# The attention's inputs loaded three items deep instead of four

## The chip, the cores and the metric

The kernel runs on one core of a Trainium2 chip. That core has a matrix engine (PE, with its weight loads shown apart as PEld), a vector engine (DVE), a scalar engine (ACT), a general engine (POOL) and a synchronising engine (SP) which here does nothing but issue DMAs. The five run their own instruction lists and meet only at semaphores. Data move between the large off-chip memory and the on-chip SBUF by sixteen DMA engines, which all queues share. The metric is the time on the device of one execution, in microseconds; lower is better.

## The reference

Two blocks follow one another. The first is a linear attention with decay over 4 batches, 8 heads, 768 steps and head size 48:

```
state = 0                                            # (B, H, D, D)
for t in range(S):
    cur = einsum('bhd,bhe->bhde', u * k[t], v[t])
    y[t] = einsum('bhd,bhde->bhe', r[t], state + cur)
    state = w * state + einsum('bhd,bhe->bhde', k[t], v[t])
```

Its output, with the heads side by side, is `x` (4 x 768 rows of 384). The second block is a mixture of eight experts: each row gets gate logits, an expert is chosen per row (a fresh arg-max, or the expert of the row before, as a local gate says), and the row's result is `p[e] * (relu(x @ w1[e]) @ w2[e])`, with `w1[e]` of 384 x 1024 and `w2[e]` of 1024 x 384. All is float32.

## The kernel before

**Items.** The attention is cut into 16 items, numbered 0 to 15: one item is one batch and one pair of heads (`B * HP`, 4 x 4). An item's 768 steps are six chunks of 128. Each item has three inputs in SBUF: `rk` (r and k, turned, 768 KB), `kv` (k and v by token, 584 KB) and `vT` (v turned, 384 KB). `load(n)` (L191) issues these three DMAs from SP, in that order; item 0's `rk` goes in two halves (L199).

**What an item goes through.** POOL makes three products in `scale(n)` (L205): `rw` (r times the decay, L236), `ke` (k times a decay, from `kv`, L215) and `pd` (r times k, L219). For items 0 to 2, DVE makes `rw` itself. DVE makes `kw` in `keys(n)` (k times the inverse decay, L246); for items 14 and 15 POOL does that too. PE then does `added(n)` (L258, from `ke` and `v`), `scores(n)` (L297, from `rw` and `kw`), `own(n)` (L276, from `pd`), `inside(n)` (L306, with `v` of `kv`) and `before(n)` (L319, from `rw`). DVE multiplies PE's result of `own` by `vT` (L282), masks the scores (L299) and scans the states (L264). ACT copies the result out (L327), PE turns it (L338) and, at the end of each batch, ACT writes `x` to memory with a DMA of its own (L343).

**Order.** The program's order is written out by hand (`manual_schedule`), in `run` (L362): iteration n loads an item ahead, then issues `turn(n-2)`, `added(n)`, `scale(n+1)`, `inside(n-1)`, `before(n-1)`, `scores(n+1)`, `own(n)` and `keys(n+2)`, with exceptions in the first five iterations and with the routing's work in the second half. Engines run ahead of one another as far as buffers let them: `ke`, `pd` and `kw` have two buffers each, `rw` four. Since `pd` of item m+2 goes where `pd` of item m was, POOL's `pd(m+2)` comes after PE's `own(m)`.

**Buffers of the inputs.** `AHEAD` sets how many there are, which one an item takes, and how far ahead `load` runs:

```
104         self.rks, self.vTs = [None] * AHEAD, [None] * AHEAD
105         for i in range(1, AHEAD + 1):
106             self.rks[(n + i) % AHEAD] = once.tile([P, 2, NCH, P], F32, name=f"rk{i}")
109         self.kvs = [once.tile([P, 2 * VB + DP - DH], F32, name=f"kv{i}") for i in range(AHEAD + 1)]
112         for i in range(AHEAD - 1):
113             self.load(i)
114         nc.sync.dma_start(out=self.wp, in_=wp_d)
...
194         rk, vT, kv = self.rks[n % AHEAD], self.vTs[n % AHEAD], self.kvs[n % (AHEAD + 1)]
...
375             if n + AHEAD - 1 < M:
376                 self.load(n + AHEAD - 1)
```

So with four, `rk(n)` and `vT(n)` take the place of item n-4, and `kv(n)` that of item n-5. SP works its list in order: the DMA of `rk(n)` waits until POOL and DVE have done with `rk(n-4)`, `kv(n)` until PE's `inside(n-5)` is through, `vT(n)` until DVE's multiplication after `own(n-4)` is. The weights `wp` (128 KB) are loaded behind the third item (L114).

**After the attention.** The pool that holds these buffers is closed (L522) and the experts' pools are laid where it was. The first thing there is the second set of expert weights, `w1t` and `w2t` (24 KB of each partition), which lies over the four `rk` buffers and is fetched from ACT (L1593, L1104, L1106) while the first expert's rows are computed. The experts are ten blocks of gathered rows, bound by PE, to the end of the kernel.

Of the kernel before, what the change touches and what calls it, by code (L numbers as in the profile page):

```python
# [48 lines left out]

W_LO, W_HI = 0.8, 1.25  # L50
C2 = NCH // 2
AHEAD = 4
VB = NCH * 2 * DH
LATE = (B * HP - 2, B * HP - 1)

# [7 lines left out]
class Attention:  # L63
# [13 lines left out]
    def __init__(self, tc, st, rk_d, kv_d, vT_d, x_d, w_t, wp_d, kept, ident, lt, mp):  # L77
# [25 lines left out]
        n = B * HP - 1  # L103
        self.rks, self.vTs = [None] * AHEAD, [None] * AHEAD
        for i in range(1, AHEAD + 1):
            self.rks[(n + i) % AHEAD] = once.tile([P, 2, NCH, P], F32, name=f"rk{i}")
        for i in range(1, AHEAD + 1):
            self.vTs[(n + i) % AHEAD] = once.tile([P, 2, C2, P], F32, name=f"vT{i}")
        self.kvs = [once.tile([P, 2 * VB + DP - DH], F32, name=f"kv{i}") for i in range(AHEAD + 1)]
        self.items = [dict() for _ in range(B * HP)]  # L110
# [1695 lines left out]
```

## Time and profile before

| | us |
|---|---|
| median of three runs | 377.43 (377.28 to 378.89) |
| the profiled execution | 378.4 |
| its span, first to last instruction | 376.7 |
| PE busy | 361.5 |
| DVE busy | 244.8 |
| POOL busy | 152.3 |
| ACT busy | 110.5 |

The profile's page gives the busy time of each engine and, in 40 slices of 9.42 us, each engine's busy share in tenths, the clock granted to PE, and what the DMA engines moved. The trace behind it answers for any line, tile or stretch: who waited for whom, and each instruction's start and length. In a timeline row the columns are start, length, engine, source line, operation, what is written and read, shape and count; idle time before it and its releaser stand in brackets. The attention takes the first 107 us or so, the experts the rest.

### The profile page before, as it was taken

To read this page: it belongs to the slowest core of one execution; us is meant where nothing else is said; L and a number is where in the kernel's file an instruction comes from. 1 tells how busy PE (TensorE), PEld (TensorE's weight loads), DVE (VectorE), ACT (ScalarE), POOL (GpSimd) and SP (SyncE) were. 2 spreads that over 40 slices of the span, in tenths; PEclk is the share of its full clock that TensorE was granted. 3 is DMA by queue.
4 is the path that set the end of the run, shared out by engine and by line. 5 is a ranking of instruction groups with operands and counts; after the bars stand their busy time and mean duration, and the time that the engine had idled before them with its cause. 6 is when DMAs were issued, how large, how long until landed. Compare 5 with 4: busy or idle time off the path is not lost. (4 is left out here: it accounts for less than half of the span.)

```text
span 376.7 us, 9667 instructions
## 1 busy us (share of the span) xinstructions
PE 361.5 (96%) x3844; PEld 318.7 (85%) x3844; DVE 244.8 (65%) x711; ACT 110.5 (29%) x304; POOL 152.3 (40%) x212
## 2 busy tenths in 40 slices
PE   7998899999999999999999999999999999999992
PEld 6766777777769998989899999999999998989971
DVE  6887778788834835886557666857767767555300
ACT  4222232223523212322332233333243233331210
POOL 8789999789512055212333113313233023021012
PEclk9999999999999999999999999999999999999998
DMA  7999998992568748713352452264165065072011
GB/s 256 411 407 408 404 409 314 338 357 106 196 194 298 269 169 336 260 35 127 121 198 62 155 216 78 56 218 186 36 209 220 14 220 202 19 259 114 2 41 37
DMA packets 17764, 74.93 MB, mean 199 GB/s; under 512 B 2778, under 2 KB 6624, under 8 KB 15408
## 3 DMA queue, kind: packets, MB, share of 16 engines
q1 hardware_dynamic: 10336, 56.89, 40.7%
q0 software_dynamic: 3424, 9.48, 7.3%
q10 hardware_dynamic: 3952, 7.87, 5.6%
q8 instruction: 32, 0.52, 0.6%
q14 instruction: 20, 0.16, 0.1%
HBM read 64.79 MB, written 9.47 MB: 197 GB/s over the span
## 5 line engine op out<-in xcount | busy, mean ns | idle before, releaser
L1358 POOL DMA_INDIRECT out_dram<-yo,sid x27 | 26.6, 985 | 115.8 <-ACT yo L1353 92.3
L1209 PE MATMUL h<-exT,w1t 128*128 128x168 f32 (+4 forms) x240 | 54.9, 327 | 0.0
L1213 DVE TENSOR_TENSOR hT<-h,hs 128x168 f32<-128x168 f32 (+3 forms) x60 | 21.1, 351 | 46.2 <-PE h L1209 29.6
L1132 POOL DMA_INDIRECT xg<-x_d,gid x29 | 31.2, 1076 | 30.3 <-DVE gid L899 19.2
L1209 PEld LDWEIGHTS h<-exT,w1t 128*128 128x128 f32 x240 | 41.6, 190 | 0.3 <-issue 0.3
L1159 PE MATMUL h<-exT,w1t 128*128 128x168 f32 (+2 forms) x192 | 37.3, 332 | 0.0
L299 DVE TENSOR_TENSOR am<-pair,kept 128x768 f32<-128x768 f32 x32 | 30.1, 953 | 11.0 <-PE pair L297 10.8
L1278 PE MATMUL y<-factors,sums 128*128 128x192 f32 x168 | 36.8, 326 | 0.0
L219 POOL TENSOR_TENSOR pd<-rk 128x384 f32<-128x384 f32 x32 | 31.8, 1014 | 8.9 <-PE y L276 6.3
L1209 PE MATMUL h<-xs,ws 128*128 128x168 f32 (+4 forms) x144 | 35.3, 327 | 0.0
L1159 PEld LDWEIGHTS h<-exT,w1t 128*128 128x128 f32 x192 | 30.9, 190 | 2.0 <-issue 0.2
L1278 PEld LDWEIGHTS y<-factors,sums 128*128 128x128 f32 x168 | 29.0, 190 | 0.2
L1209 PEld LDWEIGHTS h<-xs,ws 128*128 128x128 f32 x144 | 25.5, 190 | 4.3 <-ACT hs L1216 1.2
L297 PE MATMUL pair<-rw,kw 48*64 48x128 f32 (+1 forms) x768 | 23.4, 249 | 1.9 <-issue 1.7
L236 POOL TENSOR_TENSOR rw<-rk,tab 128x384 f32<-128x384 f32 x26 | 23.6, 930 | 0.4 <-DMA rk<-in_rk_dram 0.4
L306 PE MATMUL y<-am,kv 128*64 128x128 f32 x360 | 22.9, 276 | 0.3
L1278 PE MATMUL y<-w2t,hT 128*128 128x192 f32 x96 | 23.0, 328 | 0.0
L297 PEld LDWEIGHTS pair<-rw,kw 48*64 48x64 f32 x768 | 19.9, 133 | 3.4 <-issue 2.4
L1146 DVE COPY exT<-tp 128x384 f32<-128x384 f32 (+5 forms) x29 | 13.8, 485 | 13.2 <-PE tp L1145 13.1
L215 POOL TENSOR_TENSOR ke<-kv,endT 128x288 f32<-128x288 f32 (+1 forms) x32 | 21.8, 704 | 0.9 <-DMA kv<-in_kv_dram 0.9
L306 PEld LDWEIGHTS y<-am,kv 128*64 128x64 f32 x360 | 19.4, 137 | 2.2 <-issue 1.1
L327 ACT COPY xT<-y 128x768 f32<-128x768 f32 x15 | 12.0, 801 | 29.0 <-PE y L319 29.0
(304 smaller groups left out, 735.4 us busy)
## 6 DMA issues: line engine op xcount, KB each, us to landing
w1t<-in_w_dram SPq DMA_DIRECT2D x8, 1536.0 KB, 6.9
w2t<-in_w_dram SPq DMA_DIRECT2D x8, 1536.0 KB, 7.4
rk<-in_rk_dram SPq DMA_DIRECT2D x15, 768.0 KB, 10.3
kv<-in_kv_dram SPq DMA_DIRECT2D x16, 584.0 KB, 8.5
vT<-in_vT_dram SPq DMA_DIRECT2D x16, 384.0 KB, 6.3
x_d<-x ACTq DMA_DIRECT2D x4, 1152.0 KB
w1t<-in_w_dram SPq DMA_DIRECT2D x2, 768.0 KB
w2t<-in_w_dram SPq DMA_DIRECT2D x2, 768.0 KB, 5.2
```

What stands on the lines that cost most here:

```text
L215: nc.gpsimd.tensor_mul(t["ke"][:, z], t["k"][:, z], spread(self.endT[:, p, hp], 1, len(range(NCH)[z])))
L219: nc.gpsimd.tensor_mul(t["pd"][:, z], t["rT"][:, z], t["kT"][:, z])
L236: engine.tensor_mul(t["rw"][:, z], t["rT"][:, z], spread(pw, 1, z.stop - z.start))
L297: nc.tensor.matmul(sc[f * DP:(f + 1) * DP, h, i, x:], lhsT=t["kw"][q, c, o * DP:(o + 1) * DP], rhs=t["rw"][q, c, x:], start=True, stop=True)
L299: return lambda: nc.vector.tensor_mul(t["am"][:, g], sc, spread(self.kept[:, g:g + 3], 1, 2))
L306: nc.tensor.matmul(t["y"][h][p * DP:(p + 1) * DP, c2 * P:(c2 + 1) * P], lhsT=t["v"][:, (2 * c + h) * DH:(2 * c + h) * DH + DP], rhs=t["am" ...
L1132: self.nc.gpsimd.indirect_dma_start(out=xg[:n], out_offset=None, in_=self.x_d[:rows], in_offset=bass.IndirectOffsetOnAxis(ap=u["gid"][:n, ...
L1159: nc.tensor.matmul(h[:, :n], lhsT=u["w1"][:, m, kk, :], rhs=u["xT"][:, kk, :], start=(kk == 0), stop=(kk == DK - 1))
L1209: nc.tensor.matmul(out, lhsT=a, rhs=b, start=start and k == 0, stop=stop and k == len(terms) - 1, skip_group_check=True)
L1213: nc.vector.tensor_tensor(out, a, b, op=Alu.add)
L1278: return lambda: nc.tensor.matmul(bank[:, x * half:(x + 1) * half], lhsT=a, rhs=b, start=(j == 0 and x == 0), stop=(j == FK // 2 - 1), ski ...
L1358: self.nc.gpsimd.indirect_dma_start(out=out.rearrange("n (h d) -> (n h) d", h=2) if half else out, out_offset=bass.IndirectOffsetOnAxis(ap ...
```

## The change

One constant is changed:

```
-AHEAD = 4
+AHEAD = 3
```

By the lines above this does five things. There are three `rk` and three `vT` buffers in place of four, and four `kv` in place of five. `rk(n)` and `vT(n)` now follow item n-3, and `kv(n)` item n-4. Before the loop two items are loaded in place of three, so that `wp` stands on SP's list ahead of item 2, not behind it. In iteration n, `load(n+2)` is issued in place of `load(n+3)`. And each partition has 13.6 KB less in that pool (6144 + 3072 + 4672 bytes), so that what follows in it lies lower, and the second set of expert weights lies over three `rk` buffers and two of `vT`. The number of DMAs, their sizes and their order, `wp` apart, stay; so do all instructions of the other engines.

## The prediction

> **What bounds the kernel now.** I read the page first, then a table of stretches, then the waits, then the timeline of SP, POOL and PE. The page:
>
> ```profile
> span 376.7 us, 9667 instructions
> PE   7998899999999999999999999999999999999992
> GB/s 256 411 407 408 404 409 314 338 357 106 196 194 298 269 169 336 260 35 127 121 198 62 155 216 78 56 218 186 36 209 220 14 220 202 19 259 114 2 41 37
> ```
>
> PE is busy to nine tenths nearly throughout. The change touches only the loads of the attention, slices 0 to 10. There the loads move some 408 GB/s until slice 5 ends (56 us). Two stretches of it, with all engines:
>
> ```profile
> core 0: us, PE busy (x) PEld busy (x) DVE busy (x) ACT busy (x) POOL busy (x), PEclk, DMA share, GB/s
> 36.20:62.50 26.30, 24.43 (x587) 19.41 (x587) 19.22 (x42) 7.35 (x20) 24.09 (x30) 1.00 1.01 395
> 62.50:88.00 25.50, 25.01 (x551) 19.34 (x547) 21.43 (x36) 7.04 (x16) 21.22 (x26) 1.00 0.80 293
> ```
>
> PE works 93% and 98% of them, POOL 92% and 83%; the DMA engines are full in the first and 80% busy in the second. PE sets the pace of 5 to 7 us per item, and POOL is not far from it. So the question is whether later inputs make PE wait. The waits of SP's queue and of POOL tell who waits for inputs today:
>
> ```profile
> SPq L201 <- DVE y L282: 24.7, 9, 3.6
> SPq L200 <- PE y L306: 9.7, 6, 4.6
> SPq L201 <- DMA rk<-in_rk_dram: 5.4, 4, 1.5
> POOL pd L219 <- PE y L276: 6.3, 5, 2.4
> POOL pd L219 <- DMA rk<-in_rk_dram: 2.4, 2, 1.4
> POOL ke L215 <- DMA kv<-in_kv_dram: 0.9, 1, 0.9
> POOL rw L236 <- DMA rk<-in_rk_dram: 0.4, 1, 0.4
> ```
>
> SP waits for buffers (the first two rows), early on also for earlier DMAs to land (the third). No PE or DVE row of size names an input. Only POOL waits for inputs: 3.7 us in four waits, all before 27 us. Later POOL waits for PE, because `pd` has two buffers: POOL is ahead of PE and gives its lead up there.
>
> **The change, part by part.** No instruction is added or removed; all cost is in when the loads start.
>
> *Early items (3 to 8).* These are SP's issues of `rk` that matter, and a last reader of item 2's buffer:
>
> ```profile
> 18.36 0.38 SPq L196 DMA_DIRECT2D rk<-in_rk_dram  x1
> 19.67 0.55 DVE L236 TENSOR_TENSOR rw<-rk,mp 128x384 f32<-128x384 f32 x1
> 26.40 0.33 SPq L196 DMA_DIRECT2D rk<-in_rk_dram  x1
> 31.71 0.33 SPq L196 DMA_DIRECT2D rk<-in_rk_dram  x1
> 36.62 0.38 SPq L196 DMA_DIRECT2D rk<-in_rk_dram  x1
> ```
>
> These are items 5, 7, 8 and 9. After the change item 5 waits for item 2's reader, until 20.22: 1.9 us later. Item 7 waits for item 4's, which is the row at 31.71: 5.3 us later. Do these delays reach the data? Landing times, for the issues at 26.4, 31.7 and 58.0 in that order:
>
> ```profile
> DMA to landing us min/median/max: 11.7/11.7/11.7
> DMA to landing us min/median/max: 10.7/10.7/10.7
> DMA to landing us min/median/max: 5.7/5.7/5.7
> ```
>
> The last queue is nearly empty, so 5.7 us is an `rk` behind its predecessor's `vT` alone; the others stood some 6.0 and 5.0 us behind earlier loads. An issue that comes later by less than that finds the same place in the same stream and lands at the same time: 1.9 and 5.3 are below 6.0. Item 8 goes from 31.71 to the slot at 36.62, 4.9 us later, against 5.0. So up to about 42 us data land as before. `wp`, now ahead of item 2, costs that item 128 KB at 408 GB/s, an estimated 0.3 us; POOL's wait of 0.4 us for item 3 takes it up. Sum so far: 0 (at most 0.3).
>
> *From item 9 on, one slot later.* SP's slots are set by the readers (24.7 and 9.7 us above): `vT` and the next `rk` leave when a multiplication at L282 ends. Unless the compute moves, the slots stay and each carries one item less: the slot that took `rk(10)` takes `rk(9)`. Nothing stands ahead then. The slots, and when POOL, the first reader, wants the data:
>
> ```profile
> 46.85 0.39 SPq L196 DMA_DIRECT2D rk<-in_rk_dram  x1
> 52.69 1.69 POOL L236 TENSOR_TENSOR rw<-rk,tab 128x384 f32<-128x384 f32 x2
> 58.01 0.38 SPq L196 DMA_DIRECT2D rk<-in_rk_dram  x1
> 64.14 1.69 POOL L236 TENSOR_TENSOR rw<-rk,tab 128x384 f32<-128x384 f32 x2
> 72.03 0.68 SPq L200 DMA_DIRECT2D kv<-in_kv_dram  x1
> 78.33 1.36 POOL L215 TENSOR_TENSOR ke<-kv,endT 128x288 f32<-128x288 f32 x2
> ```
>
> With 5.7 us: item 9 is there at 52.55 (wanted 52.69), item 11 at 63.7 (64.14). Just in time, both. The slot in the last pair, which takes `kv(13)` in place of `kv(14)`, is the worst, since ACT's write of `x` goes beside the loads from 65 us on. It landed in
>
> ```profile
> DMA to landing us min/median/max: 9.1/9.1/9.1
> ```
>
> So `kv(13)` is there at 81.1, 2.8 us late: **POOL will wait**, some 3 us around 78 us. What does that cost PE?
>
> *The cover.* POOL's lead over PE, and a stretch with the columns of the table above:
>
> ```profile
> 81.55 1.98 POOL L219 TENSOR_TENSOR pd<-rk 128x384 f32<-128x384 f32 x2 [1.85 <-PE y L276]
> 86.58 0.66 PE L258 MATMUL mp<-kv,ke 128*48 128x48 f32 x20
> 93.54 1.96 POOL L246 TENSOR_TENSOR kw<-rk,held 128x384 f32<-128x384 f32 x2
> 97.73 1.27 PE L297 MATMUL pair<-rw,kw 48*64 48x128 f32 x46
> ```
>
> ```profile
> 81.55:95.50 13.95, 13.95 (x296) 10.44 (x296) 11.70 (x23) 5.61 (x16) 13.95 (x16) 1.00 0.42 149
> ```
>
> PE reads `ke(13)`, which POOL has at 79.7 (78.33 + 1.36), at 86.6: a lead of 6.9 us, so 2.8 us late doesn't reach PE there. What runs on in POOL's list is the lateness itself: at 81.55 POOL waits 1.85 us for PE anyway, which takes 2.8 down to about 1.0. From there POOL is without a pause (13.95 of 13.95 us) up to `kw(15)`, ready at 95.5, read by PE at 97.7: a lead of 2.2 us, against 1.0 late. Sum: 0.
>
> DVE reads `rk` after POOL does, in `keys(n)` at the end of iteration n-2; `vT(n)` has three items' time. Neither wants data sooner than POOL.
>
> *Behind the attention.* The second set of expert weights now lies over three `rk` and two `vT`. The last multiplication with any `vT`, and ACT's fetch into that memory:
>
> ```profile
> 102.86 1.17 DVE L282 TENSOR_TENSOR pair<-pair,vT 128x384 f32<-128x384 f32 x2 [0.25 <-PE pair L276]
> 114.68 0.36 ACTq L1104 DMA_DIRECT2D w1t<-in_w_dram  x1
> ```
>
> The readers are done 10 us before; cost 0.
>
> *The sum* is 0 on the profiled execution, 376.7 us of span in 378.4 (1.7 us outside the span, untouched). That execution is 1.0 us over the median of three, so the forecast is the median: 377.4.
>
> Bounds of what no row shows: the landing times with shorter queues. Below, an `rk` takes 5.7 us at best; POOL would then wait less, still for nothing on PE. Above, the longest landing of a `kv` in the trace:
>
> ```profile
> DMA to landing us min/median/max: 5.7/8.5/12.2
> ```
>
> I take 5.7 without and 9.1 us with the write beside it, since those are the very slots.
>
> **Rivals.** *POOL's lead runs out (slower).* Place: `kw(15)`, or `scores(15)` at 97.7. It decides once POOL is over 1.85 + 2.2 = 4.1 us late at 78 us, which is a landing of 10.4 us for the slot at 72.03 (78.33 + 4.1 - 72.03). With the 12.2 of the full queue POOL is 5.9 us late and PE waits 1.8: 379.2. If the next slots are as slow and POOL loses about 1 us more, 380.2. For it: the slot already takes 9.1, and the lateness comes back in SP's slots, as `rk` waits for POOL. Against it: fewer loads are in the queue. The Trainium skill, "Perfetto Trace Analysis", Optimization Strategy, speaks for this rival: the same gap repeating on an engine that should be saturated can mean that buffers for the next tile lack. By that, one buffer less should open one gap per item; the rows put that gap on POOL and not on PE, and no run here yet shows it.
>
> *PE's instruction supply gains (faster).* PE has pauses in which it waits for nothing that the profile shows, here in 24 to 36 and in 36 to 62.5 us, and a queue of instructions shares the DMA engines:
>
> ```profile
> PE pair L297 <- issue: 1.2, 2, 1.0
> PE mp L258 <- issue: 1.7, 2, 1.3
> q8 instruction: 32, 0.52, 0.6%
> ```
>
> The same waits sum to 0.5 us in 62.5 to 88, where the DMA engines are less full. If the pauses are late instructions, an earlier end of the saturation (42 instead of 58 us) saves up to 1.7 us: 375.7; if all 2.9 go, 374.5. Against it: most of the pauses lie before the queue gets shorter. The Trainium skill, "DMA: Bandwidth & Descriptors", Queues, rings and completion order, speaks against it as well: each DMA engine takes its queues in turn, packet by packet, so a long queue should delay another one no more than a short one. No run here shows that.
>
> *The depth isn't in force (no change).* SP's waits for earlier DMAs (5.4 us in the row above) would pace it instead. That holds up to 26 us only; then the same 377.4 would come with unchanged landing times.
>
> **How the numbers follow.** About 0.5%, 1.9 us, is what a measurement of this kernel can tell from no change: 375.5 to 379.3. The forecast (loads one slot later, hidden by POOL's lead) has 0.75; the depth not in force 0.03, at the same time; POOL's lead running out 0.14, about 379.2 to 380.2, of which 0.01 within the bound; the gain of instructions 0.08, about half of it beyond the bound, as only the full 2.9 is past it. That makes faster 0.05, same 0.82, slower 0.13. The range leaves out the far ends of both, 0.05 and some 0.07: 375.7 to 379.7.
>
> **What would show it.** Right: landing times of `rk` near 6 us from item 8 on, where they were 10 to 12 until item 8; DMA share in 36 to 62 us below 1.0; new waits of POOL for `rk` or `kv`, some 3 to 4 us in sum after 50 us, the longest near 78; POOL's waits for PE at L219 shorter by about that much; PE's waits and the start of the experts, at 109 us, as before. Wrong: a wait of PE's L297 or L258 on POOL, and a later start of the experts; or the experts starting earlier with PE's pauses gone. A difference that arises after 109 us would be none of these, and would point to where the tiles lie.

## The result, and the profile after

| | before | after |
|---|---|---|
| median of 21 executions each, on the same chip | 377.52 us (376.46 to 381.29) | 380.49 us (376.30 to 385.54) |
| executions over 379 us | 3 of 21 | 15 of 21 |
| ratio after / before, 95% interval | | 1.0052 [1.0032, 1.0073] |
| the profiled execution | 378.4 us | 377.7 us |

The change makes the kernel about half a per cent slower (0.8% by the medians of all executions), and the forecast, 377.4 within 375.7 to 379.7, missed it. Ratios leave out single executions that stand out from their own kernel; medians, spans of times and counts here are of all. The last two rows do not fit together: the profiled execution of after is *faster* than that of before. The 21 times say why. After's lie in two groups: 376.30 to 378.60 (6 times) and 379.50 to 385.54 (15 times), with nothing in between. Before has the same upper group, seldom. The profile after is of the lower group; it shows what the depth does, and not yet the loss.

The page of after:

```profile
span 375.9 us, 9672 instructions
GB/s 249 412 409 402 298 346 317 367 341 304 181 187 317 268 147 367 249 25 157 104 199 62 173 191 65 78 234 149 41 225 212 17 229 178 33 276 83 2 42 37
```

The loads now fall below 400 GB/s from the fifth slice on (38 us) in place of the seventh. The same two stretches as before, with the busy time of each engine:

```profile
core 0: us, PE busy (x) PEld busy (x) DVE busy (x) ACT busy (x) POOL busy (x), PEclk, DMA share, GB/s
36.20:62.50 26.30, 24.95 (x595) 19.43 (x591) 20.08 (x43) 7.34 (x20) 24.92 (x31) 1.00 0.93 325
62.50:88.00 25.50, 25.42 (x555) 19.54 (x551) 20.91 (x38) 7.25 (x17) 21.72 (x26) 1.00 0.95 346
```

The DMA share went from 1.01 to 0.93 in the first and from 0.80 to 0.95 in the second: loads moved to later, as the change says. PE has lost nothing there (24.43 and 25.01 us before). The waits of POOL up to 105 us:

```profile
POOL rw L236 <- DMA rk<-in_rk_dram: 4.5, 4, 1.6
POOL pd L219 <- DMA rk<-in_rk_dram: 2.5, 2, 1.8
POOL pd L219 <- PE y L276: 1.3, 1, 1.3
POOL ke L215 <- DMA kv<-in_kv_dram: 0.9, 1, 0.9
```

POOL's wait for `rk` at L236 grew from 0.4 to 4.5 us and its wait for PE at L219 shrank from 6.3 to 1.3 us: the lead is spent on later data. PE's timeline at the first matmul of the experts, before in the first line and after in the second (start, duration, in brackets the wait):

```profile
109.25 0.85 PE L1145 MATMUL tp<-ident,xg 128*128 128x128 f32 x6 [0.47 <-DMA xg<-x_d,gid]
108.40 0.86 PE L1145 MATMUL tp<-ident,xg 128*128 128x128 f32 x6 [0.25 <-DMA xg<-x_d,gid]
```

So in this execution the experts start 0.85 us earlier. Where are the 3 us of the others?

### The profile page after: what moved, and what is told of

The parts are those of the page before. It is cut to its first block, busy times and chain, and to the rows that moved or that the text cites. A ratio compares the mean times of both kernels' runs of the same rounds, so it can differ in the third digit from the quotient of the medians.

```text
span 375.9 us, 9672 instructions
## 1 busy us (share of the span) xinstructions
PE 362.7 (96%) x3844; PEld 319.9 (85%) x3844; DVE 245.7 (65%) x711; ACT 110.3 (29%) x304; POOL 152.2 (40%) x212
## 5 line engine op out<-in xcount | busy, mean ns | idle before, releaser
L299 DVE TENSOR_TENSOR am<-pair,kept 128x768 f32<-128x768 f32 x32 | 30.1, 953 | 9.9 <-PE pair L297 9.8
L219 POOL TENSOR_TENSOR pd<-rk 128x384 f32<-128x384 f32 x32 | 31.7, 1012 | 3.8 <-DMA rk<-in_rk_dram 2.5
L236 POOL TENSOR_TENSOR rw<-rk,tab 128x384 f32<-128x384 f32 x26 | 23.8, 938 | 4.7 <-DMA rk<-in_rk_dram 4.5
L297 PE MATMUL pair<-rw,kw 48*64 48x128 f32 (+1 forms) x768 | 23.2, 249 | 1.2 <-issue 0.9
L297 PEld LDWEIGHTS pair<-rw,kw 48*64 48x64 f32 x768 | 19.8, 133 | 2.8 <-issue 1.4
```

What stands on the lines that cost most here:

```text
L219: nc.gpsimd.tensor_mul(t["pd"][:, z], t["rT"][:, z], t["kT"][:, z])
L236: engine.tensor_mul(t["rw"][:, z], t["rT"][:, z], spread(pw, 1, z.stop - z.start))
L297: nc.tensor.matmul(sc[f * DP:(f + 1) * DP, h, i, x:], lhsT=t["kw"][q, c, o * DP:(o + 1) * DP], rhs=t["rw"][q, c, x:], start=True, stop=True)
L299: return lambda: nc.vector.tensor_mul(t["am"][:, g], sc, spread(self.kept[:, g:g + 3], 1, 2))
```

## The experiments

Three theories stand at the start. A: the inputs come too late in some executions, more than the cover holds. B: it is not the loads, but where the tiles that lie behind the input buffers come to be. C: a lower clock. The change takes away one `rk` (6,144 bytes of each partition), one `vT` (3,072) and one `kv` (4,672), 13,888 bytes in all, and every tile allocated behind them moves down by that much. To vary the parts, the counts were given names of their own in L104 to L109 and L194:

```
+NRK, NVT, NKV = 3, 3, 4
-        self.rks, self.vTs = [None] * AHEAD, [None] * AHEAD
+        self.rks, self.vTs = [None] * NRK, [None] * NVT
...
-        self.kvs = [... for i in range(AHEAD + 1)]
+        self.kvs = [... for i in range(NKV)]
...
-        rk, vT, kv = self.rks[n % AHEAD], self.vTs[n % AHEAD], self.kvs[n % (AHEAD + 1)]
+        rk, vT, kv = self.rks[n % NRK], self.vTs[n % NVT], self.kvs[n % NKV]
```

Added lines shift line numbers: L830 is the same instruction as L831, L832 or L833 in some experiments below, and the other lines shift with it.

**The change again.** No edit.

> The changed kernel once more, for its own spread: its runs went from 376.3 to 385.5 us, while the profiled one (377.7) shows PE unhindered. Theory A (late inputs): in the slow executions POOL's lead runs out, PE waits for POOL or for an input before 107 us, and the experts start 2 to 5 us later than the 108.4 us of the profiled one. Theory B (where the tiles lie): the attention takes what it took, and the loss of 3 us lies after 109 us. Theory C (clock): the loss goes with a longer stretch of half clock, wherever it is. Ratio to the kernel before by all three: 1.003 to 1.008, median about 380.5.

Measured: 380.66 us (376.61 to 382.19), ratio 1.0046 [1.0010, 1.0082], 8 of 12 executions over 379. This time the profiled execution is one of them, 380.3 us. Its PE waits around the end of the attention, and what PE does there:

```profile
93.35 0.88 PE L276 MATMUL y<-pd,w_t 48*64 48x384 f32 x8
96.49 0.79 PE L338 MATMUL pair<-ident,xT 112*128 112x112 f32 x6 [2.27 <-DVE am L299]
```

In the profile of before the same two stand back to back:

```profile
93.62 0.88 PE L276 MATMUL y<-pd,w_t 48*64 48x384 f32 x8
94.42 0.79 PE L338 MATMUL pair<-ident,xT 112*128 112x112 f32 x6
```

PE waits 2.27 us for DVE, not for POOL and not for a load: L338 writes into the bank `pair` that DVE's L299 has still to read. Why is L299 late? DVE's timeline, first of this execution and then of before:

```profile
90.85 0.17 DVE L829 SCALAR_TENSOR_TENSOR si<-inv,eb 128x12 int32<-128x12 f32 x1
91.06 4.44 DVE L830 TENSOR_SCALAR si<-si 128x12 int32<-128x12 int32 x1
95.41 0.16 DVE L831 TENSOR_SCALAR si<-si 128x12 int32<-128x12 int32 x1
95.49 0.94 DVE L299 TENSOR_TENSOR am<-pair,kept 128x768 f32<-128x768 f32 x1
```

```profile
91.32 0.17 DVE L830 TENSOR_SCALAR si<-si 128x12 int32<-128x12 int32 x1
91.41 0.90 DVE L831 TENSOR_SCALAR si<-si 128x12 int32<-128x12 int32 x1
93.28 0.96 DVE L299 TENSOR_TENSOR am<-pair,kept 128x768 f32<-128x768 f32 x1 [0.98 <-PE pair L297]
```

L830 and L831 are a bitwise "and" and a shift on 12 numbers per partition, part of the routing of the first rows. The trace counts L830 as busy for 4.44 us, where 0.17 do. It must have been held up, and it ends when POOL ends. POOL's timeline of this execution ("x2" is two instructions, shown as one group):

```profile
90.59 1.68 POOL L236 TENSOR_TENSOR rw<-rk,tab 128x384 f32<-128x384 f32 x2
92.23 1.33 POOL L215 TENSOR_TENSOR ke<-kv,endT 128x288 f32<-128x288 f32 x2
93.53 1.94 POOL L246 TENSOR_TENSOR kw<-rk,held 128x384 f32<-128x384 f32 x2
97.84 0.83 POOL L841 TENSOR_TENSOR val<-eqv,t 128x384 f32<-128x384 f32 x1 [2.38 <-DVE eqv L836]
```

The second `kw` ends at 95.47, L830 at 95.50. From 91.06 on POOL ended five instructions with the next one right behind, and L830 got in at none of these places, only when POOL ran out of work. In before, beside the same row of POOL's work, L831 ends at 92.31, where `rw` ends and `ke` begins:

```profile
90.59 1.68 POOL L236 TENSOR_TENSOR rw<-rk,tab 128x384 f32<-128x384 f32 x2
92.24 1.34 POOL L215 TENSOR_TENSOR ke<-kv,endT 128x288 f32<-128x288 f32 x2
```

A's sign, late inputs ahead of PE, is absent. In this execution C's is absent too: its mean granted clock is 0.995, as in the profiled execution of 377.7 us. C comes back further down, behind the hold.

**The same place.** The change, with an unused tile that puts the tiles behind back where they were:

```
+        once.tile([P, 3472], F32, name="pad")      # 13,888 bytes, behind the kv tiles
```

> Three items deep, with an unused tile of 13888 bytes behind the input buffers, so that everything after them in the pool lies where it lay before. Theory A: no different from the changed kernel, ratio 1.003 to 1.008 and runs up to 381 and more. Theory B: as the kernel before, ratio 0.998 to 1.002, nearly all runs below 379.

Measured: 377.31 us (375.91 to 379.20), ratio 0.9989 [0.9968, 1.0011], 1 of 12 over 379. Three items deep costs nothing if the tiles stay where they were. The interval lies clear of the one in the result, [1.0032, 1.0073]; beside the change's second measurement, taken with this one on one chip, it is 1 execution in 12 over 379 against 8 in 12. So B holds and A falls. This profile has POOL's waits for inputs too, and DVE gets in after 0.97 us:

```profile
POOL pd L221 <- DMA rk<-in_rk_dram: 3.1, 2, 1.9
POOL ke L217 <- DMA kv<-in_kv_dram: 2.8, 4, 1.6
POOL rw L238 <- DMA rk<-in_rk_dram: 1.4, 3, 0.6
```

```profile
89.76 0.97 DVE L832 TENSOR_SCALAR si<-si 128x12 int32<-128x12 int32 x1
90.64 0.16 DVE L833 TENSOR_SCALAR si<-si 128x12 int32<-128x12 int32 x1
```

**Fewer `rk` and `vT` alone, fewer `kv` alone.** Counts of 3, 3, 5 and of 4, 4, 4 (loads issued as in the change).

> Three buffers for rk and vT as in the changed kernel, but five for kv as before. Theory A with kv as the late one (2.8 us late for POOL in the profile's slots): ratio back to 1.000. Theory A with rk as the late one: as the changed kernel, 1.003 to 1.008, since rk still follows item n-3. Theory B: between.

> Four buffers for rk and vT as before, four for kv as in the changed kernel (before: five); wp still ahead of item 2. Theory A with rk as the late one: ratio back to 0.998 to 1.002, nearly all runs below 379. Theory A with kv as the late one: still 1.003 to 1.008. If wp's place mattered, both e3 and e4 would stay slow.

Measured: 3, 3, 5 gives 377.19 us (376.80 to 382.20), ratio 0.9999 [0.9970, 1.0027], 1 of 12 over 379. With 4, 4, 4 it is 381.72 us (379.66 to 384.93), ratio 1.0101 [1.0058, 1.0143], 6 of 6 over 379: the version that gives up least has the greatest loss. By depth that makes no sense; by place it does. 3, 3, 5 moves the tiles by 9,216 bytes, 72 times 128; 4, 4, 4 by 4,672, 36.5 times 128; the change by 13,888, 108.5 times 128. What is slow is what moves them by an odd number of 64 bytes. The profile of 4, 4, 4 has the same row on DVE, and on PE, from 62 to 110 us, more than that:

```profile
94.34 3.67 DVE L831 TENSOR_SCALAR si<-si 128x12 int32<-128x12 int32 x1
```

```profile
PE y L277 <- issue: 2.1, 2, 1.5
PE pair L339 <- DVE am L300: 1.5, 1, 1.5
```

The 2.1 us in which PE waits for nothing that the profile shows are more than any other profile has on that line (at most 1.4, in the one of after with 64 bytes below), and are not explained here.

**64 bytes.** If it is the place modulo 128, then 64 bytes behind the `kv` tiles heal the change and harm the kernel before:

```
+        once.tile([P, 16], F32, name="pad")        # 64 bytes, behind the kv tiles
```

> The changed kernel with an unused tile of 64 bytes behind the input buffers. The profile of e1 lost its time where one small DVE instruction (L830) took 4.4 us in place of 0.2 while POOL worked without a pause; e2 and e3, free of that, have their POOL tiles at the same address modulo 128 as the kernel before, the changed kernel and e4 have them 64 off. Theory P (place within 128 bytes): ratio 0.997 to 1.002, L830 below 1 us, at most one or two executions above 379. Theory M (the 13.6 KB that moved, or the depth): ratio 1.003 to 1.008 as the changed kernel.

> The kernel before (four items deep) with the same unused tile of 64 bytes, so that its POOL tiles lie 64 off modulo 128. Theory P: 1.003 to 1.010, most executions 379.5 to 382, and L830 near 4 us in a slow one. Theory M: 0.998 to 1.002.

Measured: after with 64 bytes 377.52 us (376.83 to 379.66), ratio 0.9999 [0.9975, 1.0023], 2 of 12 over 379; before with 64 bytes 380.83 us (379.05 to 382.04), ratio 1.0064 [1.0025, 1.0104], 8 of 8 over 379. The whole effect of the change came from an unused 64 bytes, in a kernel four items deep. The two rows, after with 64 bytes first:

```profile
91.23 0.63 DVE L832 TENSOR_SCALAR si<-si 128x12 int32<-128x12 int32 x1
91.77 0.85 DVE L833 TENSOR_SCALAR si<-si 128x12 int32<-128x12 int32 x1
```

```profile
90.65 4.02 DVE L832 TENSOR_SCALAR si<-si 128x12 int32<-128x12 int32 x1
94.59 0.16 DVE L833 TENSOR_SCALAR si<-si 128x12 int32<-128x12 int32 x1
```

The first of these two profiles is of an execution of 379.31 us, without the hold. So an execution just over 379 need not have a hold, and the counts over 379 are not counts of holds.

**Is it L830?** Place might harm elsewhere, with the held instruction only a companion. In the next pair L829 writes its number to PSUM for the first rows, and L830 and L831 read it there; all else stays, the places too. Once in the change, once in before:

```
+        g["s0"] = one[:, E * (n + 1) + n:E * (n + 1) + 2 * n].bitcast(I32)
...
+        s0 = g["s0"] if i == 0 else g["si"][:, 0]
-        nc.vector.scalar_tensor_tensor(g["si"][:, 0], g["r"], ...)
-        nc.vector.tensor_scalar(g["si"][:, 1], g["si"][:, 0], P - 1, ...)
-        nc.vector.tensor_scalar(g["si"][:, 2], g["si"][:, 0], 7, ...)
+        nc.vector.scalar_tensor_tensor(s0, g["r"], ...)
+        nc.vector.tensor_scalar(g["si"][:, 1], s0, P - 1, ...)
+        nc.vector.tensor_scalar(g["si"][:, 2], s0, 7, ...)
```

> The changed kernel, places as they are, but the number that L830 and L831 read stands in PSUM (free columns of the lent bank) in place of SBUF, so that they have no use for a second SBUF port. Theory L (L830 held up by POOL is the loss): L830 and L831 take under 0.3 us in every case, ratio 0.995 to 1.000, no more executions at 380 to 382. If the loss has another cause that comes with the place: still 1.003 to 1.008.

> The kernel before with the same edit. Theory L: 0.995 to 1.000, its own few executions at 379 to 381 gone; L831, 0.9 us in the profile of before, then 0.2. Otherwise 1.000 with the spread of before.

Measured: the change with it 377.75 us (376.42 to 379.49), ratio 1.0002 [0.9975, 1.0030], 2 of 12 over 379; before with it 377.58 us (376.85 to 379.30), ratio 1.0006 [0.9978, 1.0033], 3 of 12. The tiles of the change lie at the bad place here, and the upper group is gone: nothing beyond 379.49, where the change alone went to 382.19. Before with it keeps executions of 379.1 to 379.3, against what was expected, but has none over 380, where 5 of the 31 executions of before beside it were. Both instructions are short in the change's profile:

```profile
90.71 0.17 DVE L833 TENSOR_SCALAR si<-inv 128x12 int32<-128x12 int32 x1
90.80 0.16 DVE L834 TENSOR_SCALAR si<-inv 128x12 int32<-128x12 int32 x1
```

**Whose place?** Behind the `kv` tiles come first the decay's tables, then, in pools of their own, `ke`, `pd`, `kw`, `am`, `S` and `rw`: POOL's products and two of DVE's. In the first of three kernels, all with before's counts, 64 bytes behind the tables move only the second lot; in the second, 64 bytes ahead of the tables and 64 behind move the tables by 64 and the products by 128; in the third only `rw` is moved by 64:

```
+        once.tile([P, 16], F32, name="pad2")       # first and second: behind the tables
+        once.tile([P, 16], F32, name="pad")        # second: also behind the kv tiles
+        self.two.tile([P, 8], F32, name="pad3")    # third: after S of item 0, two buffers of 32 bytes
```

> The kernel before with 64 unused bytes behind the tables (step, tab, end, endT): only ke, pd, kw, am, S and rw move by 64; the tables and inputs stay. If it is the place of POOL's products that decides: ratio 1.003 to 1.010, most executions over 379.5. If it is the place of the tables that POOL reads (tab, endT): 0.998 to 1.002.

> 64 unused bytes ahead of the tables and 64 more behind them: the tables move by 64, the products by 128, which is the same place modulo 128 (though not modulo 256 or 512). Products decide, modulo 128: 0.998 to 1.002. Tables decide, or the products' place modulo 256: 1.003 to 1.010.

> Only rw moves by 64 (unused bytes at the end of the pool ahead of it). When L830 waits, POOL makes rw, ke and kw of item 15. If one product out of place is enough: 1.003 to 1.010 or half of it, L830 up to 1.7 us, the length of rw's pair. If all must be out of place, so that no gap between POOL's instructions lets L830 in: 0.998 to 1.002.

Measured: products moved by 64: 380.35 us (379.33 to 381.10), ratio 1.0055 [1.0034, 1.0076], 7 of 7 over 379. Tables by 64 and products by 128: 377.62 us (376.77 to 378.57), 0.9985 [0.9962, 1.0007], 0 of 12. `rw` alone: 377.22 us (376.16 to 380.71), 0.9982 [0.9967, 0.9997], 1 of 13. So it is the products (with DVE's `am` and `S`, which moved along), modulo 128 bytes, and `rw` by itself does not bring the loss. DVE's row with the products moved by 64, by 128, and with `rw` moved, in that order:

```profile
90.72 4.32 DVE L832 TENSOR_SCALAR si<-si 128x12 int32<-128x12 int32 x1
```

```profile
91.16 0.17 DVE L833 TENSOR_SCALAR si<-si 128x12 int32<-128x12 int32 x1
```

```profile
90.80 4.18 DVE L833 TENSOR_SCALAR si<-si 128x12 int32<-128x12 int32 x1
```

The last is a stroke of luck: of the 13 executions with `rw` moved the profiled one was the one over 379, 380.71 us, and it has the hold. So the hold can happen with `ke` and `kw` at the good place; `rw` was not, and no profile shows a hold with all of them there. That before's own 3 of 21 are the same event is likely, but none of them was profiled.

**A better version.** Three deep at before's places (13,888 bytes of padding), with the number in PSUM.

> Three items deep, places as in the kernel before (e2), and the number of L830 in PSUM (e7): whether the two together beat the kernel before. Held up no more and no deeper than need be: 0.996 to 1.000. If the port was all, no better than e2's 0.999.

Measured: 377.30 us (376.69 to 378.64), ratio 0.9976 [0.9954, 0.9997], 0 of 12 over 379. It is better than the change; against before the interval barely leaves 1, no more than that of `rw` alone, [0.9967, 0.9997], which has no remedy in it. So a gain over before is not shown.

**The clock again.** After the hold PE's clock is not always what it was. The rows of the granted clock, of the change again and of the products moved by 64:

```profile
PEclk9999999999999999999999999999999999999998
PEclk9999999999899999999999999999999999999998
```

The 8 is the slice from 94.8 to 104.2 us. Taken microsecond by microsecond, the clock with the products moved is 1.00 up to 95 us, where PE stands still, and 0.50 from 96 to 99. The profiles of before with 64 bytes and of `rw` moved show the same within 96 to 101 us; those of the change again and of 4, 4, 4 have the hold and no drop, and the nine profiles without the hold are nines up to the last slice. So in these profiles the drop comes behind PE's pause and cannot be what caused it, but it can be a part of the loss: of all executions over 380 us of the change and the experiments 29 of 36 have a mean clock of 0.992 or less, of those below 379 us 5 of 97. How much of the time it costs was not separated.

In seven profiles, the hold and what follows from it:

| | L830 | PE's wait for L299 at L338 | experts start | span | start to end |
|---|---|---|---|---|---|
| before | 0.17 us | none | 109.25 | 376.7 | 267.5 |
| after, profiled | 0.41 | none | 108.40 | 375.9 | 267.5 |
| after, same place | 0.97 | none | 107.42 | 374.3 | 266.9 |
| after with 64 bytes | 0.63 | none | 110.06 | 377.6 | 267.5 |
| after again | 4.44 | 2.3 | 111.31 | 378.6 | 267.3 |
| products by 64 | 4.32 | 2.1 | 112.08 | 379.0 | 266.9 |
| 4, 4, 4 | 3.67 | 1.5 | 115.04 | 382.0 | 267.0 |

The last column is span less start: what comes after the experts' start takes the same time in all within 0.6 us, so the loss arises ahead of them.

## Why the prediction was wrong

**Early items, and one slot later: right.** In the lower-group profile the loads of `rk` issued from 30 to 90 us land so, before in the first line and after in the second:

```profile
DMA to landing us min/median/max: 5.7/7.7/10.7
```

```profile
DMA to landing us min/median/max: 5.9/6.7/9.0
```

The 5.7 taken for an empty queue was near the minimum of 5.9, and the longest fell from 10.7 to 9.0. POOL waits after 50 us, in its timeline:

```profile
59.18 1.99 POOL L236 TENSOR_TENSOR rw<-rk,tab 128x384 f32<-128x384 f32 x2 [1.15 <-DMA rk<-in_rk_dram]
72.15 2.01 POOL L236 TENSOR_TENSOR rw<-rk,tab 128x384 f32<-128x384 f32 x2 [1.56 <-DMA rk<-in_rk_dram]
78.35 1.69 POOL L236 TENSOR_TENSOR rw<-rk,tab 128x384 f32<-128x384 f32 x2 [0.78 <-DMA rk<-in_rk_dram]
```

That is 3.5 us in sum, with 3 to 4 forecast. The place was a miss: the longest is at 72 us and for `rk`, not at 78 for `kv(13)`. The `rk` loads issued at 63.0 and 70.0 us took 9.0 and 8.3 us, and the prediction had weighed only `kv(13)` there.

**The cover: right.** POOL's lead took the lateness up: PE's wait for POOL's `pd` at L276 is 0.3 us in the profile after, where it was 1.0 before. The depth alone is worth 0.9989 [0.9968, 1.0011]. The sum of 0 was right for what it summed.

**The step that failed** is the opening sentence of the change's part, "No instruction is added or removed; all cost is in when the loads start", with *Behind the attention*, where place was weighed for the second expert weights only and given cost 0. A buffer count also moves every tile allocated behind it. What stood at 0 was 3.0 us in the medians (377.52 to 380.49). Here 13,888 bytes are an odd number of 64, which moved POOL's products to the other half of 128 bytes; there the executions over 379 us go from 3 in 21 to 15 in 21. In the five profiles with the hold of L830, PE waits 1.5 to 2.3 us behind it; in three of them the clock's drop, and in 4, 4, 4 PE's other pauses, come on top. The runs: 64 bytes put in harm before (1.0064 and 1.0055), 64 put in heal the change (0.9999), and with L830's input in PSUM the bad place does no harm (1.0002). The sign given at the end of the prediction, a difference after 109 us, was wrong as well: place shows ahead of it, at 91 to 96 us.

**The rivals.** *POOL's lead runs out* named nearly the right time, 379.2 to 380.2, by the wrong mechanism: the lead did not run out. *PE's instruction supply* did not gain: in the profile after the pauses of L258 and L297 sum to 2.2 us where they were 2.9, and no gain clear of the noise shows in the time at the same place (0.9989 [0.9968, 1.0011]). *The depth not in force* fell with the landing times.

**What the profile before could have shown.** L831 stands there with 0.90 us where L830, of the same form and size, takes 0.17. Two equal instructions with unequal durations were here a wait that the profile counts as work, beside POOL's `rw`, which ends as L831 does. It could not have shown how often it becomes 4 us.

## What to carry to other kernels

A change of a buffer count is two changes: depth, and the place of all that is allocated behind. Test them apart with an unused tile of the size that was taken away. Look at the spread of many executions and profile one of each group: one profile of the quick group explains nothing of a loss that comes in two executions of three. Where a short DVE instruction from SBUF to SBUF stands beside an unbroken row of POOL's work and others queue behind it, its input in PSUM kept it free here.

## What the runs showed of the hardware

A DVE instruction of 0.17 us took 4.0 to 4.4 us beside POOL's stream in four profiles (3.7 with 4, 4, 4), past four or five ends of POOL's instructions. In three of these five profiles the granted clock fell to 0.50 for some 3 us right after PE's pause of 1.8 to 2.1 us; in the other two, with pauses of 2.3 and 1.5 us, it stayed at 1.00. The Trainium skill, "SBUF — State Buffer", Who interferes with whom, says that a `tensor_scalar` of DVE in a two-port mode and GpSimd's instructions take a shared port pair as a lock, one whole instruction at a time, and that the other blocks fully meanwhile. The trace of before agrees: L831 took 0.90 us and ended with POOL's `rw`. A hold over four or five instructions in a row, and one that depends on 64 bytes of the place of POOL's tiles, is more than that section states; the measurements above stand for it. The Trainium skill, "VectorE: DVE Perf Modes", Why PSUM operands drop a tier, says that an operand in PSUM shuts the two-port modes out; by that L830 with its number in PSUM should never wait for POOL, and in the profiles it took 0.17 us, also at the bad place.

Open are why POOL hands the pair over at one place and not at the other, whether `ke`, `kw`, DVE's `am` or all of them together decide (only `rw` alone was tried), whether it is their own place or their place relative to `si`, which no padding moved, what other places than these two, 64 bytes apart, would do, why the clock falls behind some holds only, and the further 2.1 us of PE's pauses with 4, 4, 4. That the hold is a port held by POOL is argued from the timeline and from the remedy in PSUM; the port itself shows in no view.
